# Eight small moves in a fused three-stage kernel: weight asks, a clamp, a table of casts, a weight load and four stores

## The chip, the cores and the metric

The kernel runs on one core of a Trainium2 chip. Its time is the device time of one execution, in microseconds (us); below 1 us the profile gives parts of a microsecond or ns. The core has a matrix engine (TensorE, PE in the profile; PEld is its loading of stationary operands), a vector engine (VectorE, DVE), a scalar engine (ScalarE, ACT), a general engine (GpSimd, POOL) and SyncE (SP), which here only asks for transfers and reads tables into registers. Transfers between the chip's main memory and the core's SBUF are made by 16 DMA engines; SP and GpSimd ask for them, GpSimd for those with an index per row (gathers and scattered stores).

## The reference

Three models follow each other. A linear attention over 4 sequences, 8 heads and 768 tokens comes first (the kernel takes 64 tokens as a chunk, and a pair of chunks, 128 tokens, as a unit):

```python
log_a = np.log(np.clip(a, 1e-06, 1.0))
cum = np.cumsum(la, axis=-1)                       # inside one chunk
L = np.exp(cum[:, :, :, None] - cum[:, :, None, :]) * causal
M = np.einsum('bhin,bhjn->bhij', Cc, Bc) * L
y = einsum('bhij,bhjd->bhid', M, xc) + einsum('bhin,bhnd->bhid', Cc, state) * exp(cum)
state = exp(sum(la)) * state + sum(Bx * exp(cum[-1:] - cum))
```

Its output, 3072 rows of 256, goes through a mixture of 8 experts in which each row takes the one with the largest gate (`h = relu(x[mask] @ w1[e])`, `out[mask] = gate * (h @ w2[e])`; w1 is 256 x 1024, w2 is 1024 x 256), and the result through a second mixture of 4 experts of the same size, in which every row passes all four, weighted by given probabilities:

```python
for e in range(4):
    out += p[:, e:e + 1] * (np.maximum(x @ w1[e], 0.0) @ w2[e])
```

## The kernel before, in words

All products are float32 in two parts: a high part `hi` rounded to the matrix engine's format and the remainder `lo`, so weights are cast (ScalarE, L160) and subtracted (GpSimd, L166) after they are loaded (`load_w`, L143). The four compute engines run instructions in the order in which the program emits them (`manual_schedule`).

**Stage 1, 0 to about 87 us.** 24 units pass the loop `for i in range(NU + 1)`. Unit by unit: decay products by a scan on VectorE (`decay`, Lt, L476); `br`, the B rows times a decay, on GpSimd (L484); scores `cb` on TensorE (L497) and `M` on VectorE (L499); `Cs`, C times a decay, on GpSimd (L558); `within` and `across`, the two parts of y (L511, L523); `yT`, ScalarE's copy of y (L529); `tp`, a product that transposes it (L569); copies and a store to `xs` in main memory (L577 to L579); `gain`, a product U for the state (L544); and the state's scan (L553). Inputs `xb` come for two units at a time (`load`, L436), and their off-diagonal parts are filled with zeros (`blank`, L445). C and B come for three units at a time into one of three buffers `cz` (L338): C twice, with zeros in the heads that are not taken, and B, 576 KB in one transfer. The input a is clamped in two halves (L393), the second on GpSimd. Between units stand the routing of the rows to the 8 experts, and the weights of expert 0 in four tiles (two of w1, two of w2), each loaded in four pieces (pieces of a tile of w2 are rows, casts take columns).

At the end GpSimd fetches rows of `xs` by index (`gather`, L291): two tiles early (`ie`), then the other two of expert 0 (`idx`), then those of expert 1 (`idr`); TensorE transposes each (`tpx`, L304). The first products of expert 0 (`pha`) come right behind.

**Stage 2, to about 251 us**: 8 experts; expert 0 goes first, the others by a table `tab` that VectorE makes and SP reads into registers (L969, L975) to find their weights. **Stage 3, to 766 us**: four experts, 4 row tiles (t) of 768 rows, each by 4 blocks (i) of 256 hidden units, with seven half-size products in place of eight, 384 columns wide (`hidden`: x, y, z, w are PSUM banks; s1, s5, s7 copies on ScalarE; u2, c12, c21, c22, g sums; `between(n)` puts other work at marked places: `x_sum` and `x_split` make the next tile's sums `ts` and parts `xc`, and `store_out` writes a finished row tile on GpSimd). The last expert's stores are 24 scattered transfers; the tail to 776.1 us is the last of these.

SP has eight semaphores for its transfers, and each transfer waits for the one eight before it.

Of the kernel before, what the change touches and what calls it, by code (L numbers as in the profile page):

```python
# [43 lines left out]
def body(tc, I, out):  # L44
    nc = tc.nc
    with ExitStack() as outer:
# [266 lines left out]
        with ExitStack() as ctx:  # L313
# [16 lines left out]
            def load_bc(i):  # L330


                src = I["cb"][i // 2, i % 2].rearrange("p (m s) -> p m s", m=3)
                cm = lp.tile([P, 4, HB], F32, tag="cm", name="cm")
                BC[i] = cm

                def part(a=0, e=HB):
                    nc.sync.dma_start(cz[i % NBC][:, :, a:e], src[:, :, a:e])  # L338

                def head(h, a=0, e=HB):  # L340
                    nc.scalar.activation(cm[:, h, a:e], cz[i % NBC][:, h % 2, a:e], AF.Copy, scale=hmask[:, h // 2:h // 2 + 1])

                return part, head
# [43 lines left out]
            def chunk_products(h):  # L387
# [4 lines left out]
                def ready():  # L392
                    (nc.gpsimd if h else nc.vector).tensor_scalar(a2[:, s], a2[:, s], 1e-6, 1.0, op0=ALU.max, op1=ALU.min)  # L393
# [312 lines left out]
            chunks[3]()  # L706
            for u in range(4, NXB):
                blank(u)
# [16 lines left out]
            stage, fetch = {}, []  # L725
            for m in range(2, NU // 3):
                stage[max(3 * m - 7, 0)] = m
            ws, gathers = [], []
            WEIGHTS = {2: (0, 0), 6: (0, 1), 10: (1, 0), 14: (1, 1)}
            SPLITS = {6: (0, 0), 10: (0, 1), 14: (1, 0), 18: (1, 1)}  # L730
            DECAYS = {max(3 * m - 2 - 2 * (m > 5), 2): m for m in range(1, NU // 3)}
            CHUNKS = {1: 4, 2: 2, 3: 5}
            for i in range(NU + 1):
# [7 lines left out]
                if i in WEIGHTS:  # L741
                    fetch += load_w(0, *WEIGHTS[i], pieces=4)
                for f in fetch[:1]:
                    f()
                fetch = fetch[1:]
# [4 lines left out]
                if i in SPLITS:  # L750
                    ws += split_w(0, *SPLITS[i], 4)
# [21 lines left out]
                for f in ws[:2]:  # L773
                    f()
                ws = ws[2:]
# [20 lines left out]
                if i < 2:  # L796
                    nc.gpsimd.memset(pfg[i + 2], 0.0)
                slot(2)
# [129 lines left out]
        with ExitStack() as ctx:  # L928
# [95 lines left out]
            for j in range(2):  # L1024
                load_w(1, 0, j)
# [3 lines left out]
            others()  # L1029
            for k in range(2):  # L1030
# [192 lines left out]
        def hidden(g, t, i, between):  # L1223
# [27 lines left out]
            product(2)  # L1251
            sc.copy(s7, bank["w"])  # L1252
            between(-1)
            if (g, t, i) != (E1, 0, 0):
                nc.gpsimd.tensor_add(g_, s5, s7)  # L1255
# [14 lines left out]
            if (g, t, i) == (E1, 0, 0):  # L1270
                v.tensor_add(g_, s5, s7)
# [66 lines left out]
        for e in range(E2):  # L1338
            g = E1 + e
            for t in range(NTP):  # L1340
                tn = (t + 1) % NTP if (e, t) != (E2 - 1, NTP - 1) else None
                for i in range(4):
# [9 lines left out]
                    def between(n):  # L1352
# [6 lines left out]
                        if n in ((1, 2) if i == 3 else (1, 3)):  # L1359
# [58 lines left out]
```

## Time and profile before

| | |
|---|---|
| runs of the kernel before | 776.25, 777.19, 778.91 us (median 777.19) |
| the profiled execution | 778.04 us, span 776.1 us |
| busy share of the span | TensorE 97%, VectorE 72%, GpSimd 61%, ScalarE 54% |
| granted clock of TensorE, mean | 0.993 |
| DMA | 46.55 MB, mean 60 GB/s |
| DMA share of the first six slices (19.4 us each) | 0.7 0.7 0.8 0.4 0.2 0.5 |

The busy share is that of matmuls in the trace. The granted clock is the share of full speed (1.00 is 2.4 GHz, 0.50 is 1.2 GHz). An entry such as "[1.54 <-POOL Cs L558]" in a timeline says that the engine had stood idle for 1.54 us, and that what it waited for last was GpSimd's Cs of line 558. "issue" means that no wait that the profile knows ended there.

### The profile page before, as it was taken

Reading aid. Unit: us, or ns where it says so; the run is one execution under the profiler, and the core shown is the slowest. Engines: PE = TensorE matmul, PEld = TensorE weight load, DVE = VectorE, ACT = ScalarE, POOL = GpSimd, SP = SyncE. Lnnn points to the kernel's source line nnn. Section 1 sums busy time; section 2 is a strip of 40 time slices with the busy share of each in tenths; the row PEclk is TensorE's granted clock in tenths of the full one; section 3 lists DMA queues with packets and bytes.
Section 4 is the critical chain, followed back from the end, with each engine's and each line's share of the span. In section 5 each row is a group of like instructions: output and inputs, shape, how many; then the busy total and the mean of one; then the engine's idle time right before and its main releaser. Section 6 shows DMA issues by size and latency. Waiting matters only on the chain.

```text
span 776.1 us, 16852 instructions
## 1 busy us (share of the span) xinstructions
PE 752.2 (97%) x6510; PEld 711.6 (92%) x6510; DVE 556.5 (72%) x988; ACT 415.2 (54%) x931; POOL 470.9 (61%) x558
## 2 busy tenths in 40 slices
PE   8998899999999999999999999999999999999994
PEld 6665698999999899999999999999999999999994
DVE  7788736664466886778867778777687887868753
ACT  7766344444554655465564555555455566454540
POOL 5656558548762754577763558865366786455434
PEclk9999999999999999999999999999999999999997
DMA  7784255434333100011100001100001100000001
GB/s 190 204 226 143 55 171 190 133 117 137 123 96 97 28 29 1 1 29 29 28 28 1 1 2 39 43 2 28 1 2 28 29 1 1 8 35 21 22 28 55
DMA packets 35746, 46.55 MB, mean 60 GB/s; under 512 B 4432, under 2 KB 25296, under 8 KB 35664
## 3 DMA queue, kind: packets, MB, share of 16 engines
q1 hardware_dynamic: 31248, 37.27, 16.1%
q0 software_dynamic: 3360, 7.13, 2.9%
q8 instruction: 52, 0.85, 0.5%
q10 hardware_dynamic: 1056, 1.05, 0.4%
q14 instruction: 30, 0.25, 0.1%
HBM read 39.10 MB, written 6.34 MB: 59 GB/s over the span
## 4 chain that ended last, share of the span: by engine, by line
PE 63%; POOL 2%; issue 1%; ACT 1%; DVE 0%; POOLq 0%; ACTq 0%
PE po L1303 34%; PE x L1235 9%; PE z L1235 8%; PE w L1235 8%; PE y L1235 4%; POOL out L1323 1%; ACT s L1248 0%; POOL ts L849 0%; ACT xc L858 0%; POOL xc L859 0%; PE poA L1303 0%; POOLq L1414 0%; POOL g L1255 0%; POOL gap L1328 0%; DVE c L1272 0%
## 5 line engine op out<-in xcount | busy, mean ns | idle before, releaser
L1303 PE MATMUL po<-w,h 128*128 128x256 f32 x2280 | 280.1, 281 | 0.3 <-DVE h L1244 0.3
L1303 PEld LDWEIGHTS po<-w,h 128*128 128x128 f32 x2280 | 277.6, 188 | 0.5 <-DVE h L1244 0.5
L1241 ACT ACTIVATE h<-c 128x384 fp32r<-128x384 f32 x192 | 98.7, 525 | 152.8 <-DVE c L1277 78.5
L1255 POOL TENSOR_TENSOR g<-s,s 128x384 f32<-128x384 f32 x63 | 63.9, 1015 | 152.6 <-ACT s L1252 151.7
L1244 DVE SCALAR_TENSOR_TENSOR h<-c,h 128x384 fp32r<-128x384 f32 x192 | 144.2, 761 | 10.9
L1257 DVE TENSOR_TENSOR u<-y,s 128x384 f32<-128x384 f32 x64 | 35.5, 555 | 68.8 <-ACT s L1252 67.5
L166 POOL TENSOR_TENSOR wl<-raw,wh 128x256 fp32r<-128x256 f32 x72 | 55.5, 796 | 42.0 <-ACT wh L160 39.3
L1235 PE MATMUL x<-xc,wh 128*128 128x384 f32 x256 | 66.9, 342 | 3.0 <-ACT s L1248 2.1
L1235 PE MATMUL w<-xc,wh 128*128 128x384 f32 x256 | 65.7, 337 | 0.5 <-DVE xc L859 0.5
L1235 PE MATMUL z<-xc,wh 128*128 128x384 f32 x256 | 65.4, 336 | 0.0
L1277 DVE TENSOR_TENSOR c<-u,g 128x384 f32<-128x384 f32 x63 | 58.8, 933 | 0.0
L1248 ACT COPY s<-x 128x384 f32<-128x384 f32 x64 | 30.6, 478 | 50.6 <-PE x L1235 50.5
L897 ACT ACTIVATE hh<-ph 128x216 fp32r<-128x216 f32 (+8 forms) x69 | 33.2, 488 | 43.0 <-PE ph L274 33.4
L859 POOL TENSOR_TENSOR xc<-x,xc 128x384 fp32r<-128x384 f32 x28 | 32.6, 1164 | 37.1 <-ACT xc L858 36.9
L1244 DVE SCALAR_TENSOR_TENSOR h<-x,h 128x384 fp32r<-128x384 f32 x64 | 35.7, 557 | 23.7 <-ACT h L1241 23.5
L859 POOL TENSOR_TENSOR xc<-ts,xc 128x384 fp32r<-128x384 f32 x46 | 52.4, 1150 | 0.0
L899 DVE SCALAR_TENSOR_TENSOR hl<-ph,hh 128x216 fp32r<-128x216 f32 (+8 forms) x69 | 37.2, 549 | 16.9 <-ACT hh L897 15.1
L274 PE MATMUL ph<-xh,wh 128*128 128x480 f32 (+8 forms) x142 | 48.6, 342 | 0.6 <-ACT hx L265 0.4
L1235 PEld LDWEIGHTS x<-xc,wh 128*128 128x128 f32 x256 | 42.3, 188 | 6.7 <-ACT s L1248 5.2
L918 PE MATMUL po<-hh,wh 128*128 128x480 f32 (+8 forms) x142 | 48.3, 340 | 0.0
L274 PE MATMUL ph<-xh,wl 128*128 128x480 f32 (+8 forms) x142 | 47.7, 336 | 0.0
L274 PE MATMUL ph<-xl,wh 128*128 128x480 f32 (+8 forms) x142 | 47.6, 335 | 0.0
(244 smaller groups left out, 1674.7 us busy)
## 6 DMA issues: line engine op xcount, KB each, us to landing
raw<-in_w SPq DMA_DIRECT2D x26, 512.0 KB, 3.9
raw<-in_v SPq DMA_DIRECT2D x32, 256.0 KB, 2.5
xb<-in_xb SPq DMA_DIRECT2D x22, 192.0 KB, 5.0
cz<-in_cb SPq DMA_DIRECT2D x7, 576.0 KB, 4.9
xs<-xo SPq DMA_DIRECT2D x24, 128.0 KB, 3.2
raw<-in_w SPq DMA_DIRECT2D x16, 128.0 KB, 3.3
raw<-in_w ACTq DMA_DIRECT2D x2, 512.0 KB, 3.9
cz<-in_cb SPq DMA_DIRECT2D x3, 192.0 KB
```

The costliest lines, as they stand in the source:

```text
L166: ins = nc.gpsimd.tensor_sub(lo[:, :, a:a + n], raw[:, :, a:a + n], hi[:, :, a:a + n].bitcast(F32))
L274: mm = nc.tensor.matmul(ph, w[:, k, fs], x[k], start=(i == 0), stop=(i == 5))
L859: eng.tensor_sub(o[:, 1], src, o[:, 0].bitcast(F32))
L899: i1 = nc.vector.scalar_tensor_tensor(hl, ph, 0.0, hh.bitcast(F32), op0=ALU.max, op1=ALU.subtract)
L918: mm = nc.tensor.matmul(po, w[:, f % 4, ks], h, start=(i == 0), stop=(i == 23))
L1235: nc.tensor.matmul(bank[to], w[:, a], x[:, r], start=(m == 0 and to not in seen), stop=(m == 2), skip_group_check=True)
L1241: sc.activation(HP[n][0], src, AF.Relu)
L1244: v.scalar_tensor_tensor(HP[n][1], src, 0.0, HP[n][0].bitcast(F32), op0=ALU.max, op1=ALU.subtract)
L1255: nc.gpsimd.tensor_add(g_, s5, s7)
L1257: v.tensor_add(u2, bank["y"], s1)
L1277: v.tensor_add(c22, u2, g_)
L1303: nc.tensor.matmul(two[h], x[:, ts], w2[:, w, j], start=(i, j, h * (len(hs) - 1), m) == (0, 0, 0, 0), stop=(i, j, m) == (3, 1, 2), skip_gr ...
```

## The change

It consists of these parts, with the lines of the program before.

1. The clamp of the second half (L393) goes from GpSimd to VectorE, and with its two small steps moves from ahead of the loop to the loop's first turn; the blanks of xb tiles 4 and 5 go to the ends of the first two turns.
2. C and B of a buffer's second use and later are loaded without C's zero halves: two transfers over every other partition, 384 KB, in place of one of 576 KB.
3. Expert 0's weight pieces are asked for, and cast, by two tables, ASKS and CASTS. Before: one ask in each turn from 2 to 17, one cast in each from 6 to 21. Now: one ask in turns 2, 4, ..., 12 and two in each of 14 to 18; one cast in 7, 9, 11, 13, 15 to 18, 22 and 23, two in 19 to 21.
4. The second weight tile of expert 1 is loaded behind expert 0's first products and the table's loads.
5. In `hidden`, `between(-1)` stands ahead of the copy s7, and the first block's g goes from VectorE to GpSimd.
6. In the last expert's blocks with i = 3 the stores go from places 1 and 2 to 3 and 4 (four stores in all).

```diff
--- before.py
+++ after.py
@@ -335,7 +335,11 @@
                 BC[i] = cm
 
                 def part(a=0, e=HB):
-                    nc.sync.dma_start(cz[i % NBC][:, :, a:e], src[:, :, a:e])
+                    if i < NBC:
+                        nc.sync.dma_start(cz[i % NBC][:, :, a:e], src[:, :, a:e])
+                        return
+                    for m in range(2):
+                        nc.sync.dma_start(cz[i % NBC][m::2, m::2 - m], src[m::2, m::2 - m])
 
                 def head(h, a=0, e=HB):
                     nc.scalar.activation(cm[:, h, a:e], cz[i % NBC][:, h % 2, a:e], AF.Copy, scale=hmask[:, h // 2:h // 2 + 1])
@@ -390,7 +394,7 @@
                 a3 = a2.rearrange("p (k i) -> p k i", k=NK)
 
                 def ready():
-                    (nc.gpsimd if h else nc.vector).tensor_scalar(a2[:, s], a2[:, s], 1e-6, 1.0, op0=ALU.max, op1=ALU.min)
+                    nc.vector.tensor_scalar(a2[:, s], a2[:, s], 1e-6, 1.0, op0=ALU.max, op1=ALU.min)
                     nc.gpsimd.tensor_copy(d1[:, k, 0:1], a3[:, k, 0:1])
                     nc.gpsimd.memset(a3[:, k, 0:1], 0.0)
 
@@ -703,9 +707,6 @@
             for u in (2, 3):
                 blank(u, True)
             decayed_b(0)
-            chunks[3]()
-            for u in range(4, NXB):
-                blank(u)
             warm(2)
             scores(0)
             decay(1)
@@ -722,14 +723,17 @@
             heads = {0: [lambda h=h: bc_next[1](h) for h in range(2)]}
             soon = {0: [lambda h=h: bc_head(h, 2 * P, HB) for h in range(2, 4)],
                     1: [lambda h=h: bc_next[1](h) for h in range(2, 4)]}
-            stage, fetch = {}, []
+            stage = {}
             for m in range(2, NU // 3):
                 stage[max(3 * m - 7, 0)] = m
-            ws, gathers = [], []
-            WEIGHTS = {2: (0, 0), 6: (0, 1), 10: (1, 0), 14: (1, 1)}
-            SPLITS = {6: (0, 0), 10: (0, 1), 14: (1, 0), 18: (1, 1)}
+            ws, steps_w, gathers = [], [], []
+            TILES = ((0, 0), (0, 1), (1, 0), (1, 1))
+            ASKS = {**dict.fromkeys(range(2, 14, 2), 1), **dict.fromkeys(range(14, 19), 2)}
+            CASTS = {**dict.fromkeys((7, 9, 11, 13, 15, 16, 17, 18, 22, 23), 1), 19: 2, 20: 2, 21: 2}
+            asks = [f for t in TILES for f in load_w(0, *t, pieces=4)]
+            splits = list(TILES)
             DECAYS = {max(3 * m - 2 - 2 * (m > 5), 2): m for m in range(1, NU // 3)}
-            CHUNKS = {1: 4, 2: 2, 3: 5}
+            CHUNKS = {0: 3, 1: 4, 2: 2, 3: 5}
             for i in range(NU + 1):
                 if i % 2 == 0 and has(i + 4):
                     load(i + 4)
@@ -738,17 +742,18 @@
                     bc[0]()
                     for k in range(2):
                         heads[3 * stage[i] - 4 + k] = [lambda h=h, bc=bc: bc[1](h) for h in range(2 * k, 2 * k + 2)]
-                if i in WEIGHTS:
-                    fetch += load_w(0, *WEIGHTS[i], pieces=4)
-                for f in fetch[:1]:
+                for f in asks[:ASKS.get(i, 0)]:
                     f()
-                fetch = fetch[1:]
+                asks = asks[ASKS.get(i, 0):]
                 if i == 6:
                     nc.sync.dma_start(dpr, I["dp"].rearrange("p (u e) -> p u e", u=NU))
                 if i == 9:
                     queue += probs
-                if i in SPLITS:
-                    ws += split_w(0, *SPLITS[i], 4)
+                for _ in range(CASTS.get(i, 0)):
+                    if not ws:
+                        ws = split_w(0, *splits.pop(0), 4)
+                    steps_w += [ws[:2]]
+                    ws = ws[2:]
                 if has(i):
                     state(i)
                 slot()
@@ -770,9 +775,10 @@
                     decays_c(DECAYS[i])
                 if has(i + 1):
                     decayed_c(i + 1)
-                for f in ws[:2]:
-                    f()
-                ws = ws[2:]
+                for fs in steps_w:
+                    for f in fs:
+                        f()
+                steps_w = []
                 if 5 <= i < 8:
                     (counts, places_first, sums_of_ones)[i - 5]()
                 for f in gathers[:1]:
@@ -795,6 +801,7 @@
                     f()
                 if i < 2:
                     nc.gpsimd.memset(pfg[i + 2], 0.0)
+                    blank(i + 4)
                 slot(2)
                 if has(i + 1):
                     gain(i + 1)
@@ -1021,12 +1028,12 @@
             gather(0, (2, 3), xs, idx)
             turns()
             experts()
-            for j in range(2):
-                load_w(1, 0, j)
+            load_w(1, 0, 0)
             hs = gemm1x(0, 0, CAP0, far=3, done_f=HA)
             slots()
             gather_turn(1)
             others()
+            load_w(1, 0, 1)
             for k in range(2):
                 nc.gpsimd.memset(x2[k][:, CAP0:2 * TB], 0.0)
             gemm2x(0, [HA.get(f, t) for f, t in enumerate(hs)], 0, CAP0, slice(0, CAP0),
@@ -1249,10 +1256,9 @@
             product(1)
             sc.copy(s5, bank["z"])
             product(2)
+            between(-1)
             sc.copy(s7, bank["w"])
-            between(-1)
-            if (g, t, i) != (E1, 0, 0):
-                nc.gpsimd.tensor_add(g_, s5, s7)
+            nc.gpsimd.tensor_add(g_, s5, s7)
             product(3)
             v.tensor_add(u2, bank["y"], s1)
             between(0)
@@ -1268,7 +1274,6 @@
             v.tensor_add(c21, bank["w"], u2)
             high("21", c21)
             if (g, t, i) == (E1, 0, 0):
-                v.tensor_add(g_, s5, s7)
                 v.tensor_add(c22, u2, g_)
                 high("22", c22)
             low("12", c12)
@@ -1356,7 +1361,7 @@
                             sums_pair(g, 3)
                         if n == 0 and g == E1 and step in (1, 2):
                             split_pair(g, step + 1, nc.vector if step == 1 else nc.gpsimd)
-                        if n in ((1, 2) if i == 3 else (1, 3)):
+                        if n in ((3, 4) if i == 3 else (1, 3)):
                             store_out()
                         if tn is not None:
                             if i < 2 and n in (0, 2):
```

The orders of the engines follow, the old one and the new one, at three places. GpSimd at the start, before (br_145 is unit 0's br, br_146 unit 1's, spare holds the clamped input, pfg a unit's decay factors):

```order
L484 TENSOR_TENSOR br_145<-xb_147,Lt 128x2x64
L393 TENSOR_SCALAR spare<-spare 64x384
L394 COPY spare<-spare 64x6
L395 MEMSET spare 64x6
L445 MEMSET xb_149 64x256 x4
L484 TENSOR_TENSOR br_146<-xb_147,Lt 128x2x64
L558 TENSOR_TENSOR Cs<-cz_131,pf 128x256 x2
L797 MEMSET pfg_152 128x288
```

and after:

```order
L488 TENSOR_TENSOR br_145<-xb_147,Lt 128x2x64
L488 TENSOR_TENSOR br_146<-xb_147,Lt 128x2x64
L562 TENSOR_TENSOR Cs<-cz_131,pf 128x256
L398 COPY spare<-spare 64x6
L399 MEMSET spare 64x6
L562 TENSOR_TENSOR Cs<-cz_131,pf 128x256
L803 MEMSET pfg_152 128x288
L449 MEMSET xb_149 64x256 x2
L488 TENSOR_TENSOR br_145<-xb_148,Lt 128x2x64
```

Both `br` and the first `Cs` come together now; the clamp and the four blanks are gone from between them, and the copy of clamped values stands ahead of the second `Cs`. Two blanks come behind the next `pfg`, the other two behind the one after it.

GpSimd at the end of stage 1, before (wl is the low part of a weight tile, xg a gathered tile, br_146 the last unit's):

```order
L558 TENSOR_TENSOR Cs<-cz_132,pf 128x256
L166 TENSOR_TENSOR wl_0_1_1587<-raw_0_1_1268,wh_0_1_1586 128x4x64
L291 DMA xg<-xs,ie 128x256
L629 TENSOR_TENSOR before<-before,red 128x8
L484 TENSOR_TENSOR br_146<-xb_149,Lt 128x2x64
L558 TENSOR_TENSOR Cs<-cz_132,pf 128x256
L291 DMA xg<-xs,ie 128x256
```

and after:

```order
L562 TENSOR_TENSOR Cs<-cz_132,pf 128x256
L166 TENSOR_TENSOR wl_0_1_1806<-raw_0_1_276,wh_0_1_1805 128x4x64 x2
L291 DMA xg<-xs,ie 128x256
L633 TENSOR_TENSOR before<-before,red 128x8
L488 TENSOR_TENSOR br_146<-xb_149,Lt 128x2x64
L562 TENSOR_TENSOR Cs<-cz_132,pf 128x256
L166 TENSOR_TENSOR wl_0_1_1806<-raw_0_1_276,wh_0_1_1805 128x4x64
L291 DMA xg<-xs,ie 128x256
L166 TENSOR_TENSOR wl_0_1_1806<-raw_0_1_276,wh_0_1_1805 128x4x64
```

Two subtractions stand ahead of the first of these gathers where one stood, and another ahead of the second; one comes behind it.

SP at the start of expert 0, before (raw_1_0 and raw_1_1 are the tiles of w1 of expert 1, raw_2 its w2 or the next expert's):

```order
L975 TENSOR_LOAD tab
L975 ISA x2
L143 ISA
L143 DMA raw_1_0_2132<-in_w 128x2x512
L143 ISA
L143 DMA raw_1_1_2134<-in_w 128x2x512
L969 TENSOR_LOAD tab
L969 ISA x12
L143 ISA
L143 DMA raw_2_0_2687<-in_w 128x2x512
```

and after:

```order
L982 TENSOR_LOAD tab
L982 ISA x2
L143 ISA
L143 DMA raw_1_0_2137<-in_w 128x2x512
L976 TENSOR_LOAD tab
L976 ISA x12
L143 ISA
L143 DMA raw_1_1_2288<-in_w 128x2x512
L143 ISA
L143 DMA raw_2_0_2692<-in_w 128x2x512
```

The second tile stands behind the table load of line 969, which is 976 in the new program. TensorE's order is the same in both.

## Rows read from the trace of the kernel before

**Rows 1.** page, busy time, share and instructions of each engine
```profile
PE 752.2 (97%) x6510; PEld 711.6 (92%) x6510; DVE 556.5 (72%) x988; ACT 415.2 (54%) x931; POOL 470.9 (61%) x558
```

**Rows 2.** stretches: us, busy (instructions) by engine, granted clock, DMA share, GB/s
```profile
62.00:82.00 20.00, 18.61 (x487) 11.99 (x488) 19.05 (x43) 11.69 (x41) 13.10 (x20) 1.00 0.35 100
```

**Rows 3.** waits of TensorE: total us, times, longest us
```profile
PE x L1235 <- ACT s L1248: 2.1, 3, 0.7
...
PE tp L569 <- ACT yT L529: 1.8, 2, 1.4
...
PE y L523 <- POOL Cs L558: 1.5, 1, 1.5
...
PE tpx L304 <- issue: 1.1, 1, 1.1
```

**Rows 4.** timeline, TensorE, 13 to 18: start, us; [idle before <-releaser]
```profile
13.05 0.44 PE L523 MATMUL y<-Cs,S 32*32 32x128 f32 x8 [1.54 <-POOL Cs L558]
...
17.66 0.43 PE L544 MATMUL U<-xb,br 128*32 128x64 f32 x16
```

**Rows 5.** timeline, GpSimd, 8 to 15
```profile
8.61 1.51 POOL L393 TENSOR_SCALAR spare<-spare 64x384 f32<-64x384 f32 x1
...
10.58 1.35 POOL L445 MEMSET xb<- 64x256 f32 x4
...
14.75 0.41 POOL L484 TENSOR_TENSOR br<-xb,Lt 128x128 f32<-128x128 f32 x1 [0.80 <-DMA xb<-in_xb]
```

**Rows 6.** stretches, columns as in rows 2
```profile
14.00:17.00 3.00, 3.00 (x45) 1.70 (x41) 1.39 (x3) 2.53 (x7) 1.38 (x3) 0.50 0.70 202
...
57.00:62.00 5.00, 3.61 (x110) 2.48 (x103) 2.93 (x6) 3.44 (x13) 3.08 (x7) 1.00 0.80 246
```

**Rows 7.** timelines, ScalarE and the weight asks of SP, 53 to 58
```profile
53.30 0.60 SPq L143 DMA_DIRECT2D raw<-in_w  x1
...
57.78 0.40 ACT L160 CAST wh<-raw 128x256 fp32r<-128x256 f32 x1 [1.19 <-DMA xb<-in_xb]
```

**Rows 8.** timelines, GpSimd and TensorE, 80 to 89
```profile
80.26 0.73 POOL L166 TENSOR_TENSOR wl<-raw,wh 128x256 fp32r<-128x256 f32 x1 [0.59 <-ACT lg L577]
...
83.82 0.99 POOL L291 DMA_INDIRECT xg<-xs,ie  x1 [0.16 <-issue]
...
88.14 0.55 PE L304 MATMUL tpx<-ident,xg 128*128 128x128 f32 x3 [0.37 <-DMA xg<-xs,ie]
```

**Rows 9.** timelines, SP and GpSimd, 95 to 97
```profile
95.24 1.00 SPq L143 DMA_DIRECT2D raw<-in_w  x2
...
95.92 0.95 POOL L291 DMA_INDIRECT xg<-xs,idx  x1 [0.30 <-issue]
```

**Rows 10.** DMA, 97.75 to 99.5: packets, MB, share of 16 engines
```profile
q1 hardware_dynamic: 300, 0.58, 96.6%
...
q0 software_dynamic: 2, 0.00, 0.1%
```

**Rows 11.** timelines, ScalarE, VectorE and TensorE, 253 to 260
```profile
253.79 0.52 ACT L858 CAST xc<-ts 128x384 fp32r<-128x384 f32 x1
...
257.34 0.54 DVE L1271 TENSOR_TENSOR g<-s,s 128x384 f32<-128x384 f32 x1
...
255.61 0.44 PE L1235 MATMUL w<-xc,wh 128*128 128x384 f32 x1 [0.50 <-DVE xc L859]
```

**Rows 12.** timelines, GpSimd and VectorE, 657 to 759
```profile
693.16 1.04 POOL L859 TENSOR_TENSOR xc<-ts,xc 128x384 fp32r<-128x384 f32 x1
...
692.95 1.67 DVE L859 TENSOR_TENSOR xc<-x,xc 128x384 fp32r<-128x384 f32 x1 [0.99 <-ACT xc L858]
...
661.33 0.56 DVE L859 TENSOR_TENSOR xc<-x,xc 128x384 fp32r<-128x384 f32 x1 [1.00 <-ACT xc L858]
...
758.00 0.56 DVE L1244 SCALAR_TENSOR_TENSOR h<-c,h 128x384 fp32r<-128x384 f32 x1
```

**Rows 13.** page, DMA issues: count, KB each, us from issue to landing
```profile
xb<-in_xb SPq DMA_DIRECT2D x22, 192.0 KB, 5.0
```

## The prediction

> **What bounds the kernel now.** I read the busy times first: TensorE works 752.2 of the 776.1 us of the span [rows 1]. So the change can touch only the 24 us in which TensorE stands, and the stretches in which it runs slowly. Next come the waits of TensorE, grouped by what ended them [rows 3]: 2.1 us in three waits for ScalarE's copy `s`, 1.8 us for `yT`, 1.5 us for GpSimd's `Cs`, 1.1 us that the view calls issue, at the transpose `tpx` of gathered rows. The change bears on all four. Then I went to each place in the timelines, and to the granted clock there. A change of 0.3%, some 2.3 us, is about what a measurement of this kernel can tell from none.
>
> **Part by part.** Terms are microseconds by which the end moves; a plus is a gain.
>
> *Start of stage 1: the clamp and the blanks.* GpSimd works through the clamp of the second half (1.51) and four blank fills (1.35) [rows 5] ahead of the `Cs` of unit 0. TensorE waits 1.54 for that `Cs` [rows 4], and then runs at 0.50 of its clock from 14 to 17 [rows 6], which is its level of 1.2 GHz. Now `br`, `br`, `Cs` follow each other; VectorE has the clamp behind its third decay scan, and the blanks come two per unit behind the `pfg` fills. GpSimd's copy of clamped values does wait for VectorE's clamp (ending near 12.9, since the scan ends near 12.6), and the `Cs` of unit 1 is queued behind that copy, so it ends near 13.9; nothing reads it before unit 1's `across`. What is late next is the input of unit 2: GpSimd's `br` waits for its DMA until 14.75 [rows 5]. With a `pfg` fill and two blanks still ahead of it I put that `br` at 14.85, its end at 15.25, and the state product that stood at 17.66 [rows 4] at 15.4. That is 2.2. Bounds: where the clock falls anyway, only part of the wait goes, 1.2; where unit 2's input lands earlier, the wait and the half of three slow microseconds go, 1.54 + 1.5, about 3.0. I take 2.2, the row that it rests on being the landing. The lead is kept as long as TensorE is the bound behind it.
>
> *Expert 0's weights.* A cast takes a column of its tile and so needs all four pieces of the ask, which come by rows. The last piece of the third tile is asked for at 53.30; the cast waits until 57.78 [rows 7], with `yT` behind it on ScalarE, and TensorE waits 1.39 for that `yT`, the longest of its kind [rows 3]. In the new tables every tile's last ask lies three units or more ahead of its first cast, and a unit takes some 3.1 us (from unit 0's `across` at 13.05 [rows 4] to the gathered rows at 88.14 [rows 8], by 24). I take 1.35, with 0 to 1.4 as bounds. Loading a C tile's zeros once takes 192 KB off each of five loads, 960 KB in all; TensorE waits for no C load, so I count nothing for them. A lead gained here must still pass VectorE, which works 19.05 of the 20 us from 62 to 82 [rows 2]. Its routing follows the logits of the units that come earlier too, so I let it pass.
>
> *The end of stage 1: a loss.* The casts now end at unit 23, and GpSimd subtracts with each. One subtraction more stands ahead of the last-but-one gather and another ahead of the last one, 0.73 each, with the last gather written at 83.82; its rows reach TensorE at 88.14, which has been waiting 0.37 [rows 8]. The first products of expert 0, the ranks and the table of turns follow. Nothing covers the two: -1.4. Bounds: -0.7, where one of them falls into GpSimd's own waits (0.59 ahead of a subtraction at 80.26), and -3.0, where the longer wait brings the lower clock too (below).
>
> *The second weight load of expert 1 behind the table loads.* SP asks for two tiles of 512 KB at 95.24, GpSimd writes the last gather of expert 0's second half at 95.92 [rows 9]. From 97.75 to 99.5 the hardware queue moves 300 packets and GpSimd's software queue 2 [rows 10]: the gather stands behind the weights, and TensorE waits 1.1 at `tpx` [rows 3]. With half the bytes moved some 3 us later, the gather lands about 2 us sooner, and the wait goes: 1.05. Bounds 0 and 1.1. On SP the moved load now stands behind two table loads, which wait for VectorE's routing, and ahead of the loads of the expert after; its tile is used by expert 1, behind all of expert 0's first products, and that is its cover. Were it late, expert 1 would wait for it.
>
> The Trainium skill, DMA: Bandwidth & Descriptors (Queues, rings and completion order), says that each DMA engine takes turns between the queues that have work, packet by packet. By that rule the gather would get its turn beside the weights, and the term would be 0, the sum 1.05 less. The row of 300 packets against 2 speaks against it here, and I keep the term; the rule is a rival below.
>
> *Start of stage 3.* ScalarE's copy `s7` (about the 0.52 of the cast beside it) comes behind the cast of T4 instead of ahead of it; the cast at 253.79 starts some 0.4 sooner, VectorE's half of T4 with it, and TensorE's wait of 0.50 for it goes for the most part. The sum `g` (0.54) leaves VectorE's chain [rows 11], and the first of the three waits for `s`, 0.7 [rows 3], shrinks by about that. I take 0.4 + 0.55 = 0.95. `g` goes onto GpSimd, ahead of its T sums; these come a microsecond later and feed sums of weights that are used only later. Bounds: 0.4, where `g` on GpSimd comes late for `c22`, and 1.2, where both waits go.
>
> *Four stores.* In the last expert two stores stand between GpSimd's halves of `xc`. VectorE's own half starts while the first store is being written and ends only after GpSimd's next tensor operation, which is queued right behind the store (693.16, 1.04): 1.67 instead of the 0.56 that the same line takes at 661.33, where no store is near [rows 12]. TensorE then waits 0.7 for `s`, and again a tile later: two of the three [rows 3]. With the stores behind the `xc` no tensor operation of GpSimd follows them for some 3 us. A VectorE operation that ran while a store was written with none behind it took 0.56 (758.00) [rows 12]. So both waits go: 1.4, bounds 0 and 1.4.
>
> The Trainium skill, SBUF — State Buffer (SBUF: two separate sides), calls the port pair that VectorE shares with GpSimd an exclusive lock, held for a whole instruction; by that, a store written by GpSimd could hold VectorE up wherever it stands, and the term would be 0. The 0.56 at 758.00 does not bear this out for a store alone.
>
> *Sum.* 2.2 + 1.35 - 1.4 + 1.05 + 0.95 + 1.4 = 5.55. The profiled execution took 778.04 us, 1.94 more than its span; less 5.55 that is 772.5. It lies 0.85 above the median of the runs, 777.19, so for the median I forecast 771.6. With terms between their bounds, not all at one end, 769.6 to 773.9.
>
> **The rivals.**
> *One gain is void.* The gather waits on something else than the weights, or the stores hold VectorE wherever they stand: 1.05 or 1.4 less, 772.7 to 773.0. For it: each rests on one or two places of the trace. Against it: the rows of packets and the two lengths of the same line.
> *The clock falls at the end of stage 1.* TensorE's wait for the gathered rows grows from 0.37 to about 1.8. A wait of 1.54 was followed by 0.50 of the clock for three microseconds [rows 4, 6], one of 1.39 by 1.00 all along (57 to 62) [rows 3, 6]. Half of three microseconds is lost again: 773.2.
> *The lead is swallowed.* VectorE between 62 and 82, not TensorE, sets when stage 1 ends, and its routing does not come sooner. The 2.2 and 1.35 go: 775.2. For it: 19.05 of 20 us busy; against it: TensorE is busy 18.61 there too [rows 2].
> *SP's queue: slower.* SP has eight transfers under way at most; each waits for the one eight before it. Units 14 to 18 now ask for 23 transfers instead of 17, 4.6 a unit. Landing takes 5.0 us from the issue in the median for the largest kind [rows 13], so a unit's asks take 4.6 x 5.0 / 8 = 2.9, just less than the 3.1 of a unit. If the load makes landings longer than 5.4 us, SP falls behind, and unit inputs and stores with it; from 7.3 us on (4.2 a unit, 1.1 too much, over five units 5.5) the whole gain is gone. At 8.2 us it is 4.7 a unit, 1.6 too much, over five units 8.0: 771.6 + 8.0 = 779.6. For it: weights are now pressed into fewer units; against it: the bytes of C are fewer, and most kinds land sooner than 5 us.
> *The change does not do what it says*: an order that ends up as before, 777.2.
>
> **How the numbers follow.** Main case 0.54; one gain void 0.14; clock 0.14; lead swallowed 0.10; SP's queue 0.06; nothing done 0.02. 0.3% lies at 774.9 and 779.5. The first three and some of the lead case are below: faster 0.82. Most of the lead case and the void one lie within, with a little of SP's: same 0.13. Slower 0.05. The range reaches from 769.4 to 775.4, over the lead case; above it lie SP's queue and the void change, below it the sum of the best ends.
>
> **What would show it.** Right: no wait for `Cs` near 12 and 1.00 of the clock from 12 to 18; no wait over 0.5 for `yT`; a wait of 1.5 to 2 at the first `tpx`; none at the second; only short waits for `s` and VectorE's `xc` at 0.56 in the last expert. Wrong: a wait for DMA on `br` or `cb` between 45 and 60, a clock under 1.00 where expert 0 starts, or a first gather as late after the start as before.

## The result, and the profile after

The changed kernel took 769.51 us (median of 4 runs, 769.49 to 770.77) against 776.84 for the kernel before (4 runs, 776.25 to 778.91): a ratio of 0.9905, interval 0.9884 to 0.9926. The forecast was 771.6 with a range of 769.4 to 775.4. A later set, on another chip than most of the experiments, gave 772.2 (6 runs, 771.21 to 773.19) against 777.32 (21 runs): 0.9932, interval 0.9908 to 0.9957. So the gain is 7.3 us in the first set and 5.1 in the later one, and 5.55 was forecast.

The profiled executions of the first set, 778.04 and 769.49 us, lie 8.3 us apart in their spans. TensorE runs the same instructions in the same order in both, so the starts of its instructions can be matched one by one; their growing difference says where time was gained (a minus is a loss):

| place (time before) | gained there | forecast |
|---|---|---|
| start, until unit 5 (27) | 2.42 | 2.2 |
| until unit 12 (48) | 0.16 | 0 |
| cast of the third weight tile (59) | 1.46 | 1.35 |
| end of stage 1 to the first `pha` (89) | -0.25 | -1.4 |
| ranks and first products of expert 0 (90 to 97) | 0.57 | 0 |
| second tile of gathered rows (103) | 1.27 | 1.05 |
| start of stage 3 (255 to 268) | 1.64 - 0.70 | 0.95 |
| stores of the last expert (698, 731) | 1.68 | 1.4 |

The rows add up to 8.25, 2.7 more than the forecast. TensorE's busy time is 749.9 of a span of 767.8. Its waits in the changed kernel (total us, times, longest us), beside [rows 3]:

```profile
PE y L527 <- DVE S L557: 1.5, 2, 0.8
...
PE x L1242 <- ACT s L1255: 0.6, 1, 0.6
...
PE tp L573 <- ACT yT L533: 0.4, 1, 0.4
```

The waits for `Cs` and for the gathered rows are gone, the one for `yT` is 0.4, and of three for `s` one is left. At the start, the timeline of TensorE and GpSimd, and then the stretch from 14 to 17, beside [rows 4 to 6]:

```profile
15.17 0.43 PE L548 MATMUL U<-xb,br 128*32 128x64 f32 x16 [0.46 <-POOL br L488]
...
10.52 0.73 POOL L562 TENSOR_TENSOR Cs<-cz,pf 128x256 f32<-128x256 f32 x1
...
14.71 0.41 POOL L488 TENSOR_TENSOR br<-xb,Lt 128x128 f32<-128x128 f32 x1
```

```profile
14.00:17.00 3.00, 2.54 (x63) 1.52 (x45) 3.00 (x4) 1.43 (x6) 2.78 (x9) 1.00 0.70 231
```

`Cs` of unit 0 comes at 10.52, the clock (the number behind the five engines) stays at 1.00, and GpSimd's `br` of unit 2 starts at 14.71 with no wait for its input; TensorE then waits 0.46 for it, at 15.17 against a forecast of 15.4. At 55 `tp` runs without a wait, and the gathers follow, GpSimd with the last early one, TensorE with the first and the second `tpx`, beside [rows 7 to 10]:

```profile
55.12 0.73 PE L573 MATMUL tp<-rhsT,yT 128*128 128x136 f32 x4
...
80.88 1.14 POOL L291 DMA_INDIRECT xg<-xs,ie  x1 [0.16 <-issue]
...
83.98 0.90 PE L304 MATMUL tpx<-ident,xg 128*128 128x128 f32 x4
...
97.48 0.60 PE L304 MATMUL tpx<-ident,xg 128*128 128x128 f32 x4
```

The transposes at 83.98 and 97.48 have no wait in brackets. Ahead of the first stand VectorE's `sl`, an operation on 6 columns in the routing, first in the kernel before and then in the changed one, and TensorE's wait for the state's scan, which VectorE has behind it:

```profile
83.36 0.33 DVE L633 SCALAR_TENSOR_TENSOR sl<-rank,m 128x6 f32<-128x6 f32 x1
...
78.58 1.49 DVE L637 SCALAR_TENSOR_TENSOR sl<-rank,m 128x6 f32<-128x6 f32 x1
...
81.56 0.66 PE L527 MATMUL y<-Cs,S 32*32 32x128 f32 x16 [0.65 <-DVE S L557]
```

In stage 3, VectorE's three `h` at 251, TensorE's wait behind them, and VectorE's `xc` with the store that one of them runs beside, to be held against [rows 11, 12]:

```profile
251.17 2.84 DVE L1251 SCALAR_TENSOR_TENSOR h<-c,h 128x384 fp32r<-128x384 f32 x3
...
260.97 0.44 PE L1242 MATMUL x<-xc,wh 128*128 128x384 f32 x1 [0.57 <-ACT s L1255]
...
686.56 0.56 DVE L866 TENSOR_TENSOR xc<-x,xc 128x384 fp32r<-128x384 f32 x1 [0.99 <-ACT xc L865]
...
688.28 0.96 POOL L1328 DMA_INDIRECT out<-acc,idc  x1 [0.19 <-issue]
...
688.58 0.56 DVE L866 TENSOR_TENSOR xc<-x,xc 128x384 fp32r<-128x384 f32 x1 [0.53 <-ACT xc L865]
```

`xc` takes 0.56 again, at 688.58 wholly within a store. The three `h` took 2.84 where they had taken 1.75, and TensorE has a new wait of 0.57 for `s`: a part of the gain at the start of stage 3 is given back.

### The profile page after: what moved, and what is told of

Read it like the earlier page. It is cut to its first block, busy times and chain, and to the rows that moved or that the text cites. A ratio compares the mean times of both kernels' runs of the same rounds, so it can differ in the third digit from the quotient of the medians.

```text
span 767.8 us, 16862 instructions
## 1 busy us (share of the span) xinstructions
PE 749.9 (98%) x6510; PEld 710.8 (93%) x6510; DVE 557.1 (73%) x988; ACT 415.2 (54%) x931; POOL 471.4 (61%) x558
## 3 DMA queue, kind: packets, MB, share of 16 engines
q1 hardware_dynamic: 31648, 36.29, 15.9%
q10 hardware_dynamic: 1056, 1.05, 0.5%
## 4 chain that ended last, share of the span: by engine, by line
PE 65%; ACT 1%; DVE 0%; POOL 0%; issue 0%; POOLq 0%; ACTq 0%; DVEq 0%
PE po L1308 35%; PE x L1242 9%; PE z L1242 9%; PE w L1242 8%; PE y L1242 4%; ACT xc L865 0%; POOL out L1328 0%; ACT s L1255 0%; DVE h L1251 0%; PE poA L1308 0%; POOLq L1419 0%; ACT h L1248 0%; DVE c L1270 0%; DVE u L1263 0%; DVE acc L1318 0%
## 5 line engine op out<-in xcount | busy, mean ns | idle before, releaser
L1261 POOL TENSOR_TENSOR g<-s,s 128x384 f32<-128x384 f32 x64 | 65.9, 1029 | 148.2 <-ACT s L1260 147.3
L906 DVE SCALAR_TENSOR_TENSOR hl<-ph,hh 128x216 fp32r<-128x216 f32 (+8 forms) x69 | 37.2, 549 | 16.9 <-ACT hh L904 16.3
L925 PE MATMUL po<-hl,wh 128*128 128x480 f32 (+8 forms) x142 | 47.6, 335 | 0.0
```

The lines of the kernel that those rows point to most:

```text
L906: i1 = nc.vector.scalar_tensor_tensor(hl, ph, 0.0, hh.bitcast(F32), op0=ALU.max, op1=ALU.subtract)
L925: mm = nc.tensor.matmul(po, w[:, f % 4, ks], h, start=(i == 0), stop=(i == 23))
```

## The experiments

They were run in three sets, the first two on one chip and the last (the changed kernel again, stage 3's start, g, unit 2's input) on another; the kernel before had medians of 776.5, 776.32 and 777.32 in them. The changed kernel itself was run again only in the last, so in the first two no median has one of the changed kernel beside it. Each run is read by its own trace first: by how far TensorE stands behind the first profile of the changed kernel at a place, and how that changes from one place to the next.

**The kernel before, again** (no edit).

> The kernel before, unchanged, profiled a second time. Its runs spread over 2.7 us, those of the changed kernel mostly over 0.02. Theory 1: one of the waits that the change removes varies from run to run (the cast of expert 0's third tile waiting for its pieces, 1.39 in the first profile, or the slow clock behind the wait for Cs); then this profile differs from the first in that wait, and TensorE's position differs by as much behind it, by up to 2 us. Theory 2: the spread comes from all over the program or from outside the span; then every wait is within 0.2 us of the first profile's.

776.97 us. The end lies 1.13 earlier than in the first profile, and 1.26 of it were gained at one place: the cast of the third tile runs without a wait.

```profile
56.92 0.42 ACT L160 CAST wh<-raw 128x256 fp32r<-128x256 f32 x1
```

0.41 was lost at 53 and 0.57 gained by 85. Theory 1: the wait that the new tables take away is 1.4 in one run of the kernel before and absent in the next. The waits for `Cs` (1.59) and for the second gathered tile (1.41) were there again. The 0.57 is a delay of the first profile alone: at 85.3 TensorE stood there in a wait that the view calls issue.

**The changed kernel, again** (no edit).

> The changed kernel, unchanged, again, on the chip of the experiments. In the runs so far the input of unit 2 landed anywhere from before 14.3 to 16.3, so that unit 2's state product stood at 14.8 to 17.5. Theory: the changed kernel's gain at the start is set by that landing, so its own runs spread over 1 to 2 us here, with a median of 770 to 770.8, and a profile shows the lag of TensorE against the first profile made before unit 4 or by a lower clock at the end of stage 1. Rival: 769.5 in nearly all runs, as on the first chip, and the experiments' spread came from their edits.

772.2. The spread of 2 us came as the theory said, the median is higher and the places are others: up to 71 this run is 0.33 ahead of the first profile, unit 2's input lands in time. At 71.5 it loses 0.69, in a wait that the view calls issue; by 92 it is 1.73 behind, by 126 it is 3.3 behind. Two stretches, and then the timeline of VectorE's two `om` (operands of `ip`, which makes the next gather's indices), GpSimd's operations beside them, and TensorE's wait:

```profile
83.00:84.00 1.00, 0.61 (x4) 0.56 (x4) 0.97 (x3) 0.37 (x1) 0.07 (x1) 0.80 0.65 188
...
84.00:87.00 3.00, 3.00 (x20) 2.56 (x20) 1.78 (x8) 1.03 (x3) 0.99 (x2) 0.50 0.16 46
```

```profile
89.01 1.95 DVE L236 TENSOR_TENSOR om<-iota,m 128x512 f16<-128x512 f16 x2
...
88.85 0.83 POOL L266 TENSOR_TENSOR la<-hx,ha 128x256 fp32r<-128x256 f32 x1 [3.15 <-ACT hx L265]
...
89.69 1.13 POOL L266 TENSOR_TENSOR hl<-hx,hh 128x256 fp32r<-128x256 f32 x1
...
90.28 0.27 PE L250 MATMUL ip<-ot,om 128*128 128x33 f16 x4 [1.26 <-DVE om L236]
```

Where stage 1 ends, the clock falls to 0.50 for some 3 us, and TensorE falls back by 0.6. The two `om` take 1.95 beside GpSimd's operations, as against 0.89 in the first profile, TensorE waits 1.26 and falls back by another 0.8. Over the fourteen profiles, with and without the change, the two `om` take 0.9, 1.4 or 1.95; 1.42 in both of the kernel before. Later 1.0 is lost at 102 and 0.6 at 126, with TensorE waiting for VectorE (0.36 and 0.85). All four profiles of this set lose about 1.0 at 102 and 0.5 to 2.0 near 126, and none of the earlier sets does; the kernel before was not profiled here, so it is open how much of the smaller gain of this set, 5.1, lies there. The falling clock is the second rival of the prediction. It shows in seven of the twelve profiles of the changed kernel and its variants (not in the first, nor with the casts or the second weight load early, the old tables or the early stores), and in neither of the two of the kernel before.

**No subtraction beside the last gather** (tables written short).

```diff
-CASTS = {7, 9, 11, 13, 15, 16, 17, 18, 22, 23: 1; 19, 20, 21: 2}
+CASTS = {7, 9, 11, 13, 15, 21: 1; 16, 17, 18, 19, 20: 2}
```

> The changed kernel with the cast table changed so that the last cast stands at unit 21 (two each at 16 to 20, one at 21) and no subtraction of GpSimd stands ahead of the last gather or behind it. By the prediction (two subtractions put the last gather 1.4 us later, nothing covers them) 1.1 to 1.4 us faster than the changed kernel, 768.1 to 768.4. Rival: TensorE reaches the transposes only at 84.0 in the changed kernel anyway, held by VectorE and by yT, and the gather has landed by then: within 0.3 us of 769.5. If casts come too early for their pieces, a new wait of ScalarE near 65 to 70 shows.

772.43 (770.37 to 773.77); the profile is of the slowest run. The casts came too early for their pieces, and the gathered rows are waited for again:

```profile
67.88 0.40 ACT L160 CAST wh<-raw 128x256 fp32r<-128x256 f32 x1 [1.62 <-DMA raw<-in_w]
...
75.32 0.41 ACT L160 CAST wh<-raw 128x256 fp32r<-128x256 f32 x1 [2.15 <-DMA raw<-in_w]
...
76.40 0.73 PE L573 MATMUL tp<-rhsT,yT 128*128 128x136 f32 x4 [1.31 <-ACT yT L533]
...
88.21 0.55 PE L304 MATMUL tpx<-ident,xg 128*128 128x128 f32 x3 [0.38 <-DMA xg<-xs,ie]
```

TensorE waits 1.69 and 1.31 for `yT` behind these casts; Another 2.6 had been lost by 23 already, with a wait of 1.09 at 19 and the clock at 0.50 from 19.7. From 76.4, where it stands 4.64 behind the first profile, it gains 0.77 up to the transposes at 88.2, and up to 96.4 (4.44 behind) it loses 0.57 again at `om` (1.42 here). So without the subtractions 0.8 is gained up to the transposes and 0.2 up to expert 0's products, and not 1.1 to 1.4: the first theory fails, and TensorE is held by VectorE as the rival says. Whether the subtractions have a part in the time of `om` is not shown: with them it took each of the three values.

**Three subtractions ahead of the last gather** (tables written short, the new one alone).

```diff
+CASTS = {7, 9, 11, 13, 15, 16, 17, 18, 20: 1; 19, 21: 2; 22: 3}
```

> The changed kernel with the last three casts all at unit 22, so that three subtractions (0.73 each) stand ahead of the last gather instead of one. By the prediction's uncovered gather 1.46 us slower than the changed kernel, 771.0. Rival, the cover: the gather has up to 0.7 us of slack at TensorE, so 0.7 to 1.2 us slower, 770.2 to 770.7, with a wait of TensorE for the gathered rows at the transpose.

772.37; in the trace 2.0 behind the first profile, with no wait for the gathered rows. Neither theory had the place. VectorE's `sl`, GpSimd's subtractions beside it, and TensorE's wait:

```profile
78.56 2.78 DVE L637 SCALAR_TENSOR_TENSOR sl<-rank,m 128x6 f32<-128x6 f32 x1
...
79.91 2.08 POOL L166 TENSOR_TENSOR wl<-raw,wh 128x256 fp32r<-128x256 f32 x3
...
82.83 0.66 PE L527 MATMUL y<-Cs,S 32*32 32x128 f32 x16 [1.94 <-DVE S L557]
```

`sl` took 2.78 and ended when GpSimd had done all but the last of the subtractions; in the first profile of the changed kernel it took 1.49, in the one before 0.33. The state's scan stood behind it, and TensorE waited 1.94 for that scan (0.65 in the changed kernel). So the price of subtractions at the end of stage 1 is paid through VectorE: 1.3 of the 2.0 come here. The rest came with a fallen clock and `om` at 1.95.

**Both weight tiles ahead of expert 0's products**, as before.

> The changed kernel with both weight tiles of expert 1 asked for ahead of expert 0's products, as before. If the gather of expert 0's second half stands behind the weights in the DMA engines: the wait at the transpose is back, 1.0 to 1.3 us slower, 770.5 to 770.8. If the engines share out between the queues packet by packet, so that the wait came from something else: no difference, 769.5.

771.55 (770.77 to 771.93). The wait is back:

```profile
99.20 0.55 PE L304 MATMUL tpx<-ident,xg 128*128 128x128 f32 x3 [0.54 <-DMA xg<-xs,idx]
```

0.54 there, and TensorE falls back by 0.75 in all: the first theory's direction, at 0.75 for 1.0 to 1.3. The packets of both queues from 94.5 to 97, while the weights move (packets, MB, share):

```profile
q1 hardware_dynamic: 313, 0.59, 62.4%
...
q0 software_dynamic: 110, 0.30, 32.6%
```

The gather's queue, at 110 beside 313, is held back here but not shut out; in [rows 10] it had been all but shut out, at 2 beside 300.

**The clamp and the blanks on GpSimd ahead of the loop**, as before.

> The changed kernel with the clamp back on GpSimd ahead of the loop, and the four blanks with it. Theory: the wait for Cs of unit 0 and the slow clock behind it return, and TensorE is 2.4 us later from unit 2 on; the lead was kept to the end, so the end is 2.4 us later, 771.9. Rival: the lead is swallowed between unit 16 and the end of stage 1 by VectorE, which is busy over 19 of 20 us there: under 0.5 us later, 770.0.

773.08 (10 runs, 770.85 to 774.79). TensorE's wait, and the clock of a stretch far behind it:

```profile
12.96 0.65 PE L527 MATMUL y<-Cs,S 32*32 32x128 f32 x8 [2.00 <-POOL Cs L562]
```

```profile
89.00:93.00 4.00, 4.00 (x24) 3.73 (x22) 3.38 (x16) 1.27 (x4) 0.56 (x1) 0.50 0.08 23
```

From unit 2 on TensorE is 3.3 to 3.5 behind the first profile, and it is 3.4 behind at units 5 to 20: VectorE's full stretch gave nothing of it back, and the lead is real. It is more than the 2.4 expected: the clock stood at 0.50 from 12.3 to 19.1, twice as long as in the kernel before. Then it fell again at the end of stage 1, for another 1.3.

**The old tables**, with C still loaded without its zeros.

> The changed kernel with one ask in each turn from 2 to 17 and one cast in each from 6 to 21, as before; C still without its zeros. Theory: the cast of the third tile waits for its last piece and yT behind it, TensorE stands 1.4 us near 55, and the two subtractions at the end go; 1.2 us slower, 770.7. Rival: the C loads of two thirds the size free the queue so that the pieces land sooner, and the wait does not return: within 0.3 us of 769.5.

770.97 (769.89 to 774.12); the profile is of the slowest run. ScalarE's cast, TensorE's `tp` behind it, and the clock after it:

```profile
57.00 0.41 ACT L160 CAST wh<-raw 128x256 fp32r<-128x256 f32 x1 [1.63 <-DMA raw<-in_w]
...
58.38 0.73 PE L573 MATMUL tp<-rhsT,yT 128*128 128x136 f32 x4 [1.83 <-ACT yT L533]
```

```profile
61.00:62.00 1.00, 1.00 (x28) 0.59 (x24) 0.00 (x0) 0.17 (x1) 0.30 (x2) 0.50 0.69 205
```

A wait of 1.83, then 1.4 more at half the clock: 3.2 in this run, and less in others, by the times: the lowest, 769.89, is within 0.4 of the changed kernel's best. The wait names the pieces (raw), which in [rows 7] stood under the name of another load. At the end of stage 1 this run, without the late subtractions, does as the run with early casts did: 4.60 behind at 80, 3.84 at the transposes, 4.42 behind `om`.

**C loaded with its zeros.**

```diff
-if i < NBC:
+if True:
     nc.sync.dma_start(cz[i % NBC][:, :, a:e], src[:, :, a:e])
```

> The changed kernel with every C load at 576 KB again, in one transfer, the new tables kept. The prediction counted nothing for the bytes: within 0.2 us of 769.5. Rival: 960 KB more between 10 and 60 us, at a DMA share of 0.6 to 0.9, make the pieces or the inputs of units late, and a wait for a cast, br or cb appears: 0.5 to 1.5 us slower.

770.84 (770.38 to 771.07). From unit 2 to unit 18 TensorE is never more than 0.6 behind the first profile and has no wait for a transfer between 25 and 60, and 1.5 at the end comes behind the fallen clock at 85 and `om` at 1.42. The bytes count for little by this trace.

**The stores at places 1 and 2**, as before.

> The changed kernel with the last expert's stores at places 1 and 2 again. Theory: VectorE's xc next to them takes 1.67 again instead of 0.56, TensorE waits 0.7 twice for s: 1.4 us slower, 770.9. Rival: the stores cost nothing where they stood and the two waits had gone through the earlier start: 769.5.

771.32 (771.03 to 773.79). VectorE's `xc`, and at the start of the same run GpSimd's `br` of unit 2:

```profile
688.83 1.68 DVE L866 TENSOR_TENSOR xc<-x,xc 128x384 fp32r<-128x384 f32 x1 [0.99 <-ACT xc L865]
...
16.33 1.14 POOL L488 TENSOR_TENSOR br<-xb,Lt 128x128 f32<-128x128 f32 x1 [1.95 <-DMA xb<-in_xb]
```

1.68 again, TensorE waits 0.72 and 0.71, and falls back by 0.80 and 0.97: the theory holds. The same profile, of the slowest run, had lost 2.3 at the start: unit 2's input landed at 16.3, so there the first term was 0.1 and no more (unit 2's state product at 17.52, as against 17.66 before).

**Stage 3's start as before.**

> The changed kernel with the copy s7 ahead of the T4 split again and the first g on VectorE. By the prediction 0.95 us slower than the changed kernel in the same call; from the two profiles 1.6 gained by 253 and 0.7 given back at 261, so 0.9. In the trace TensorE waits 0.5 for w near 249, 0.7 for s near 253, and no wait of 0.57 near 261. Rival: the whole 1.6 shows, since the wait at 261 is there either way: 1.6 slower.

772.78 against 772.2 for the changed kernel in the same set. The three steps are those expected: 0.50 at 254, 0.25 at 255, 0.74 at 258, and 0.69 less at 266, so 0.8 in all. A new wait of 2.27 showed at 126, on which the edit has no bearing. VectorE's operation on 8 columns, and GpSimd's four subtractions:

```profile
122.50 3.29 DVE L1004 TENSOR_SCALAR nov<-nov 128x8 f32<-128x8 f32 x1
...
122.97 2.79 POOL L166 TENSOR_TENSOR wl<-raw,wh 128x256 fp32r<-128x256 f32 x4
...
126.60 0.48 PE L274 MATMUL ph<-xh,wh 128*128 128x480 f32 x1 [2.27 <-DVE hl L906]
```

It is the pattern of `sl` again: 3.29 in place of 0.17. The next run has the same wait.

**Only g on VectorE.**

> The changed kernel with the first g on VectorE again, but s7 behind the T4 split. If both edits count, as predicted (0.4 for the order, 0.55 for g): 0.55 slower than the changed kernel. If g on GpSimd is what pushes GpSimd's T sums and so stretches VectorE's h at 251 (2.84 for three): no wait of 0.57 at 261, and the end within 0.2 us of the changed kernel.

772.18, the same as the changed kernel. TensorE waits 0.68 at 257 and not at 265: it falls back by 0.7 at the first place and makes up 0.73 at the second. The second theory: moving g to GpSimd gains nothing, the order of `s7` and the T4 split is the whole 0.8. The medians, 0.58 above the changed kernel for both edits undone and 0.02 below it for g alone, do not speak against it, but the runs of each spread over 2 us and more.

**Unit 2's input ahead of the second C load.**

> The changed kernel with the inputs of units 2 and 3 asked for ahead of the second C load (576 KB). If the landing of unit 2's input sets the gain of the start: GpSimd's br of unit 2 never waits for a DMA, in every run, and the late runs go; median 0.3 to 0.8 below the changed kernel in the same call. Rival: the C load then lands later, ScalarE's first heads of units 3 to 5 wait for it with yT behind them, and TensorE waits 1 to 1.6 for yT at 14: 0.5 to 1.5 slower.

774.8, slower by 2.6 than the changed kernel in the same set. GpSimd's `br` of unit 2, ScalarE's heads and TensorE's `tp`:

```profile
14.35 0.41 POOL L488 TENSOR_TENSOR br<-xb,Lt 128x128 f32<-128x128 f32 x1
...
14.46 1.12 ACT L345 ACTIVATE cm<-cz,hmask 128x384 f32<-128x384 f32 x2 [2.40 <-DMA cz<-in_cb]
...
14.83 0.35 PE L573 MATMUL tp<-rhsT,yT 128*128 128x136 f32 x1 [2.26 <-DMA rhsT<-in_wg]
```

The input is in time, and the C load and the gate weights `rhsT`, asked for behind it, are late: `yT` was done by 12.1, so `tp` waits for `rhsT`, not for `yT`. From 16 the clock then falls to 0.50 for some 3 us. The rival's direction, with more than its price, and by another load than it named. In two other runs, with the order of loads unchanged, the trace names `rhsT` too, at 14: 1.49 with the old tables and 1.57 with the early stores. So its landing moves from run to run as well.

## Why the prediction was right

Of the six terms four had the mechanism that the runs show, that of stage 3's start had half of it, and that of the end of stage 1 had another. The agreement is luck in part. The median of the first set lies only 0.1 above the lower end of the range: 1.7 came at the end of stage 1 and just behind it, where the forecast had a loss of 1.4 and nothing. The later set lies 0.6 above the forecast, with losses in its profile that no term has.

*The start* was right in mechanism and size: the wait and the half clock went, and GpSimd's `br` of unit 2 sets the pace next. In the first profile `br` waits for nothing but GpSimd's own fills, and not for its input; in two others the input is late by 1.40 and 1.95. What the forecast missed is how far that landing moves: with `br` at 14.3 to 16.3 the state product of unit 2 comes between 0.1 and 2.9 earlier by run, and the early ones can lose it again at once, as the run with early casts did.

*The cast of the third tile* was right at 1.46, and 0 as its lower bound was met by the second profile of the kernel before. With the clock falling behind it, it was 3.2 in the run with the old tables, above the bound of 1.4. That every tile's last ask lies three units ahead of its first cast holds for the two tiles of w2 alone (asks to turns 16 and 18, casts from 19 and 21). In w1 the last asks are in turns 8 and 14 and the first casts in 7 and 15; there the pieces are columns, so each cast needs its own piece only, asked for three turns ahead or more.

*The end of stage 1* is the step that failed: the path. "Nothing covers the two" took the last gather to be what TensorE waits for. In the changed kernel GpSimd asked for it 1.1 later than in step, not 1.46, and the rows were there just in time, at most 3.5 after the ask; in the four profiles where TensorE waits for them it got them 3.3 to 4.3 after it. What TensorE waits for is VectorE: `sl` and `m` took 1.49 and 1.21 beside GpSimd's operations (0.33 and 0.16 before). Held against the run with the old tables, it loses 0.7 at the state's scan and 0.5 at `ip`, and gets 0.4 back because the wait for the rows goes: 0.8 up to the transposes. Held against the run with the early casts and the second profile of the kernel before, the loss is 0.8 and 0.7. The 0.25 of the table is less because the first profile of the kernel before had its own delay of 0.57 there. So the term is about half of 1.4. The 0.57 behind it, where the forecast had nothing, is the time of the two `om`: 1.42 in the kernel before and 0.89 in the first profile of the changed one. It is no steady gain: when the changed kernel ran again they took 1.95.

The rival of the falling clock was the case when the changed kernel ran again, with no wait for gathered rows ahead of the fall, which the rival had given as its reason. It cost 0.6 there, and not the half of three microseconds. With a fall in seven of twelve profiles its chance, 0.14, was too low. What lets the clock fall in one run and not in the next is open.

*The second weight load*: 1.27 in the pair of profiles, 0.75 in the run that undoes it. The gather did stand behind the weights; by the rule of turns between queues (the Trainium skill, DMA: Bandwidth & Descriptors, Queues, rings and completion order) undoing it would have cost nothing. With 110 packets beside 313 in the undoing run and 2 beside 300 in the first profile, the shares lie between the rule and a closed door, and differ from run to run.

*Stage 3's start*: the sum was right, 0.95 against 0.8 to 1.0, its two parts were not: 0.8 to 0.9 for the order, and 0 for g, whose 0.7 at 253 is given back at 261. GpSimd's sums come later with g ahead of them, and VectorE's `h` took 2.84 beside them; that this makes the wait at 261 is argued and was not tried.

*The stores*: 1.4 against 1.68 between the two profiles and 1.77 in the run that undoes it, of which 1.43 are the waits themselves. The rival by which a store holds VectorE up wherever it stands is refuted: 0.56 within a store at its new place. `xc`, `sl` and the 8-column operation all ended just behind a tensor operation of GpSimd that ran beside them, by 0.03 to 0.44. The rule of the exclusive port pair, held for a whole instruction (the Trainium skill, SBUF — State Buffer, SBUF: two separate sides), goes some way to fit these rows; that VectorE comes through only after several such instructions is more than it says.

*SP's queue*, the slower rival, did not show: in the two profiles of the changed kernel no engine waits for a transfer between 20 and 60. (Its 5.0 us are the landing of loads of 192 KB [rows 13], not of the largest transfers.) *The swallowed lead* did not show: what the clamp's return cost at unit 5, 3.4, it cost at unit 20.

Of the 2.7 by which the table exceeds the forecast, 1.15 are at the end of stage 1, 0.57 at `om`, and 0.1 to 0.3 each at most of the other places. The medians of the first set lie only 7.3 apart, since the profiled run of the kernel before was itself 1.2 above its median.

## What to carry to other kernels

Count back-to-back runs of GpSimd tensor operations as a price on VectorE too, and not on GpSimd alone: an operation of VectorE of 0.2 to 0.3 us that falls into such a run may last until the run's end, and what is queued behind it waits too. Before a delayed transfer is priced, find the latest time at which its reader could start without it. Where a term rests on the landing of a transfer, one profile gives one draw: look at a second profile of the same kernel before its size is trusted.

## What the runs showed of the hardware

In the cases shown, VectorE was held by GpSimd operations that follow each other without a gap, for all of them or all but the last: an operation on 8 columns took 3.29 us beside four subtractions (2.79 together) as against 0.17 in the first profile, `sl` on 6 columns 2.78 beside `br`, `Cs` and the first two of three subtractions. A store of GpSimd (0.96) with only a memset behind it did not hold VectorE (0.56).

The granted clock fell to 0.50 for about 3 us where expert 0 starts in some runs of the same program and not in others, with waits of TensorE of about 0.4 ahead of it in the run of the changed kernel that fell, and of 0.65 and 0.41 in the one that did not. What decides it is open.

Landings move between runs of the same order of loads: unit 2's input, asked for at 8.6, was there by 14.3 in some profiles and at 15.9 and 16.3 in two; with `rhsT`, asked for at 7.6, TensorE went on at 12.8 without a wait in one profile and at 14.2 after 1.5 us in two.
